# Turning y, k and q on VectorE instead of TensorE in the later units of an mLSTM cell with a feed-forward block

## Chip, cores and metric

The kernel runs on one core of a Trainium2 chip. The metric is the device time of one execution in microseconds (us), median of several runs. The profile is one further execution, taken by the hardware profiler; TensorE appears in it as PE (matmuls) and PEld (weight loads), VectorE as DVE, ScalarE as ACT, GpSimd as POOL, SyncE as SP. A q behind a name (SPq) is the sequencer of that engine, which issues DMAs.

## The reference, cut

```python
# q, k, v, o_gate: (4, 8, 768, 40); i_gate, f_gate: (4, 8, 768)
for t in range(S):
    m_new = np.maximum(f_gate[:, :, t] + m, i_gate[:, :, t])
    f_stab = np.exp(f_gate[:, :, t] + m - m_new); i_stab = np.exp(i_gate[:, :, t] - m_new); m = m_new
    C = f_stab * C + i_stab * outer(vt, kt)          # per batch and head, 40 x 40
    n = f_stab * n + i_stab * kt
    y[:, :, t] = sigmoid(o_gate[:, :, t]) * (C @ qt) / np.maximum(np.abs(n @ qt), 1.0)
x = y.transpose(0, 2, 1, 3).reshape(3072, 320)       # heads side by side
out = ((x @ w1) * (x @ w2) @ w3) @ w_out             # 320 -> 1024 -> 1024 -> 320
```

The activations are float32. The four weight matrices come as float64 and are turned into float32 on the core.

## The kernel before

**Units and steps.** The sequence of 768 is cut into 6 chunks of 128 rows; with 4 batches that gives 24 units (`NU`), unit n being chunk n // 4 of batch n % 4. In each unit the recurrence is done in matrix form for all 8 heads (two blocks of 64 rows, called halves in the code). The main loop runs over steps s = 0 to 29. Step s does the cell work of unit s, the outputs y of unit s - 1 and the feed-forward work of earlier units.

**Turning.** Rows of q, k and v lie with time on the partitions. The scores need k and q with the head dimension on the partitions: `turn(n)` (line 267) turns both on TensorE, four 128x128 transposes each into PSUM (tile `pt`), and ScalarE copies the result into `kT` and `qT`. One turned slab holds two heads, each padded from 40 to 64 rows; the padding columns of `qbuf` and `kbuf` are zero. The feed-forward block needs y turned in the same way: `x_trans(n)` (line 367) does three transposes on TensorE (tile `px`), and ScalarE copies them into `xT`, which holds a group of four units. Since 320 is 128 + 128 + 64, the last 64 columns are first doubled by GpSimd (`twice`, line 364) so that the 64-row remainder stands in both halves of the partitions.

**Cell.** `quarter_work(s)` (line 286) runs the cell matmuls of a step into one PSUM tile, `cell`, which has one buffer of four banks: the outputs of unit s - 1 from the weighted scores and v (`ph`) and from the old state and q (`pi`), then the state update of unit s (`pc`, from k and v) and its scores (`ss`, from kT and qT). The matmuls of 64 rows by 64 columns use the four quarters of the array (`quarters`). VectorE multiplies the scores by the weights (line 324, `first_read`), updates the states and calls `outputs(s - 1)` (line 341), which ends with y (line 361).

**Feed-forward.** `up` and `up_rest` (lines 493 and 506) form x @ w1 and x @ w2 for some of the eight blocks of 128 hidden columns (PSUM tiles `pa`, `pb`), ScalarE copies pa into `a_sb` (line 513), VectorE multiplies (line 514, tile `ab`). `ffn_out` (line 516) multiplies by w3 @ w_out, which has been formed once in `w3o` (`w3_mm`, tile `wp`); the result `po` is copied by ScalarE into `o_sb` (line 521) and stored by SP's queue (line 523). `n_up` and `n_down` say how many of each a step does: one `up` in steps 3 to 6, two in steps 7 to 28; two `ffn_out` in steps 17 to 26, four in step 29. Group gr, which is units 4 gr to 4 gr + 3, begins its ups at step 9 for gr = 1 and four steps later for each next one, and uses its last two units two steps after that.

**Weights.** `fetch` (line 185) loads a piece of raw words through SP's queue into one of four `raw` buffers (a piece of w3 takes four DMAs), ScalarE scales one half of the words (line 159), and `convert` (line 212) makes float32 of them in five VectorE operations (lines 170 to 174); pieces of w3 are also turned in 32x32 blocks by VectorE (line 223). `n_cvt` says how many conversions a step does, two in steps 9 to 15, the last. `fetched < converted + 3` keeps the fetches three pieces ahead.

**Order.** TensorE runs its instructions in the order in which the program names them (`in_order`). The other engines' and queues' order is set by the scheduler of the tile framework, within the dependencies. A tile with n buffers is reused after n allocations: `pt`, `px`, `wp`, `pa`, `pb` and `po` share the four buffers of the pool `ps_m`; after step 24 the space of `cell` is given back and becomes a second pool of four, and the two pools then take turns (`mps`, line 75). SP's queue carries, in each step, the broadcast weights `pw` of unit s + 3 (line 129), k, q and v of unit s + 2 (line 119), its output gate (line 123), the fetches and, from step 17 on, the output rows. A DMA that must wait for a buffer or for data holds up what is queued behind it.

Of the kernel before, what the change touches and what calls it, by code (L numbers as in the profile page):

```python
# [1 line left out]

# [6 lines left out]
FP = mybir.dt.float32  # L9
# [7 lines left out]
def kernel(  # L17
# [71 lines left out]
    def mm(out, lhsT, rhs, start=True, stop=True):  # L89
        in_order(nc.tensor.matmul(out, lhsT=lhsT, rhs=rhs, start=start, stop=stop))  # L90
# [2 lines left out]
        in_order(nc.tensor.transpose(out, in_, ident[0:n, 0:n]))  # L93

    halves = [slice(0, L), slice(L, P)]
    quarters = ((0, 0), (1, 1), (0, 1), (1, 0))


    NB, NBQ = 4, 3
    qbuf = [const.tile([P, H, DP], FP, name=f"qbuf{i}") for i in range(NBQ)]  # L100
    kbuf = [const.tile([P, H, DP], FP, name=f"kbuf{i}") for i in range(NB)]
    vbuf = [const.tile([P, H, D1], FP, name=f"vbuf{i}") for i in range(NB)]
# [4 lines left out]
    wT = const.tile([P, NT2, BH], FP, name="wT")  # L107
    decay = const.tile([P, B * NP, NT], FP, name="decay")
    U_d = dram.tile([NT, BH, L], FP, name="U_d")

    o_t, u_t = {}, {}

    def rows(src, n):
        c, b = divmod(n, B)
        return src[b, :, c * P:(c + 1) * P, :].rearrange("h p d -> p h d")

    def load(n):
        for dst, src in ((kbuf[n % NB][:, :, 0:D], k), (qbuf[n % NBQ][:, :, 0:D], q), (vbuf[n % NB][:, :, 0:D], v)):
            nc.sync.dma_start(out=dst, in_=rows(src, n))

    def load_o(n):
        o_t[n] = io.tile([P, H, D], FP, name="o_in", tag="o_in", bufs=4)
# [119 lines left out]
    qT_t, kT_t, vw_t, before_t, y_t, x_t = {}, {}, {}, {}, {}, {}  # L242
# [22 lines left out]
                                    pattern=[[0, H], [1, L]], channel_multiplier=-1)  # L265

    def turn(n):
        for src, dst, name in ((kbuf[n % NB], kT_t, "kT"), (qbuf[n % NBQ], qT_t, "qT")):
            pt = mps([128, NP, P], "pt")
            for p in range(NP):  # L270
                transpose(pt[:, p, :], src[:, 2 * p:2 * p + 2, :].rearrange("p a b -> p (a b)"))
            dst[n] = sb.tile([128, NP, P], FP, name=name, tag=name)
            nc.scalar.copy(out=dst[n], in_=pt)
# [12 lines left out]
    def quarter_work(s, rest):  # L286


        rest()
        t = ps_c.tile([P, 4, 512], FP, name="cell", tag="cell")  # L290

        def part(j, c0, n):
            return t[:, j:j + 2, c0:c0 + NP * n].rearrange("p x (n d) -> p x n d", d=n)

        ss, pc, pi = part(0, 0, L), part(0, NP * L, D1), part(2, 0, D1)
        ph = [t[halves[x], 2 + x, NP * D1:(NP + H) * D1].rearrange("p (h d) -> p h d", d=D1) for x in range(2)]
        n = s - 1
        if 0 <= n < NU:
            pw, vt, qT = u_t.pop(n), vbuf[n % NB], qT_t.pop(n)
            before = before_t.pop(n)  # L300
            for hd in range(H):
                for x, r in enumerate(halves):
                    mm(ph[x][:, hd, :], pw[r, hd, :], vt[r, hd, :])
            for p in range(NP):
                for hip, x in quarters:
                    mm(pi[halves[x], hip, p, :], qT[halves[hip], p, halves[x]], before[x][halves[hip], p, :])
        n, first_read = s, None
        if n < NU:
            c, b = divmod(n, B)
            kt, vw = kbuf[n % NB], vw_t.pop(n)  # L310
            ends = range(2 if c < NT2 - 1 else 1)
            first, second, after = state[b]
            before_t[n] = first, second
            state[b] = after, second, first
            for p in range(NP):
                for x, e in quarters:
                    if x in ends:
                        mm(pc[halves[e], x, p, :], kt[halves[x], 2 * p + e, :], vw[halves[x], 2 * p + e, :])
            kT, qT, pw = kT_t.pop(n), qT_t[n], u_t[n]
            for p in range(NP):  # L320
                for hip, x in quarters:
                    mm(ss[halves[x], hip, p, :], kT[halves[hip], p, halves[x]], qT[halves[hip], p, halves[x]])
            pv = pw.rearrange("p (n two) t -> p two n t", two=2)
            first_read = nc.vector.tensor_tensor(out=pv, in0=ss, in1=pv, op=OP.mult)  # L324
            with tc.issue_after(first_read.ins):

                if c:
                    nc.vector.tensor_tensor(out=second, in0=pc[:, 0], in1=second, op=OP.add)
                else:
                    nc.vector.tensor_copy(out=second, in_=pc[:, 0])  # L330
                if len(ends) > 1:
                    decayed(after, second, n, 1)
                    nc.vector.tensor_tensor(out=after, in0=pc[:, 1], in1=after, op=OP.add)
        if 0 <= s - 1 < NU:
            if first_read is None:
                outputs(s - 1, pi, ph)
            else:
                with tc.issue_after(first_read.ins):
                    outputs(s - 1, pi, ph)

    def outputs(n, pi, ph):
        c, b = divmod(n, B)
        hs = slice(b * H, (b + 1) * H)
        h = sb.tile([P, H, D1], FP, name="h", tag="h")
        nc.vector.tensor_tensor(out=h.rearrange("p (n two) d -> p two n d", two=2), in0=pi,  # L345
                                in1=gT[:, c, hs].rearrange("p (n two) -> p two n", two=2).unsqueeze(3)
                                .to_broadcast([P, 2, NP, D1]), op=OP.mult)
        for x, r in enumerate(halves):
            nc.vector.tensor_tensor(out=h[r], in0=ph[x], in1=h[r], op=OP.add)  # L349
# [11 lines left out]
        nc.vector.tensor_tensor(out=y_t[n][:, 0:DM].rearrange("p (h d) -> p h d", d=D), in0=h[:, :, 0:D], in1=e,  # L361
                                op=OP.mult)

    def twice(n):
        nc.gpsimd.tensor_copy(out=y_t[n][:, DM:DM + REM], in_=y_t[n][:, KF * P:DM])  # L365
# [12 lines left out]
    GR, GC = 3, NT // 3  # L378
    TC = GC * L
    RG = GR * BH  # L380
    f_sb, a, F, U, on = (const.tile([RG, TC], FP, name=n) for n in ("f_sb", "a", "F", "U", "on"))
    w, g = f_sb, on
    M = const.tile([RG, GC + 1], FP, name="M")
    dec = const.tile([RG, GC], FP, name="dec")
# [29 lines left out]
        nc.gpsimd.memset(vbuf[i][:, :, D:D1], 1.0)  # L414
    for t in state:
        nc.gpsimd.memset(t[0], 0.0)
    nc.gpsimd.memset(pick, 0.0)

    nc.vector.tensor_reduce(out=pair, in_=ident[0:RG, 0:RG].rearrange("k (g j x) -> k j g x", g=GR, x=2), op=OP.add,
# [96 lines left out]
    def ffn_out(gr, j):  # L516
        po = mps([P, DM], "po")
        for f in range(FO):
            mm(po, ab_t[gr][j // 2][:, f, j % 2 * P:(j % 2 + 1) * P], w3o[:, f, :], start=(f == 0), stop=(f == FO - 1))
        o_sb = ffn.tile([P, DM], FP, name="o_sb", tag="o_sb", bufs=3)  # L520
        nc.scalar.copy(out=o_sb, in_=po)  # L521
        t0 = j * S + gr * P
        nc.sync.dma_start(out=out[t0:t0 + P, :], in_=o_sb)


    ups = [(0, list(range(f, f + 4)), slice(j * P, (j + 1) * P)) for f in (0, 4) for j in range(GT)]
# [12 lines left out]
    for s in range(len(n_up)):  # L539
# [8 lines left out]
        if s < NU:  # L548
            weighted(s)
            if s >= B:  # L550
                decayed(state[s % B][1], state[s % B][0], s, 0)
            if s:
                turn(s)
        if 0 <= s - 2 < NU:
            twice(s - 2)
        while turned < min(s - 2, NU):
            x_trans(turned)
            turned += 1
        fold()
# [1 line left out]
            ffn_out(*downs.pop(0))  # L561
        now = [ups.pop(0) for _ in range(n_up[s])]
        open_ups = [up(*x) for x in now]
        if len(now) < 2 and turned == s - 2 < NU:
            x_trans(turned)
            turned += 1

        def rest():
            for x in open_ups:
                up_rest(*x)  # L570

        if s <= NU:
            quarter_work(s, rest)
# [53 lines left out]
```

## Time and profile before

| | us |
|---|---|
| median of 3 runs | 494.35 (494.25 to 498.0) |
| profiled execution | 495.68 |
| its span | 494.0 |
| around the span | 1.68 |

| group in the profile | count | busy us | mean ns |
|---|---|---|---|
| PE pt, from k and from q | 192 | 33.2 | 306 and 292 |
| PE px | 72 | 13.1 | 286 |
| ACT copies kT, qT, xT | 72 | 40.1 | 588, 595, 490 |
| POOL y (the doubling) | 24 | 7.3 | 306 |
| DVE block transpose of w3, 128x512 | 16 | 11.3 | 709 |
| PE cell, all forms | 3008 | 86.0 | 235 to 238 |

| DMA, all on SP's queue | count | KB each | median us to landing |
|---|---|---|---|
| k, q, v rows | 72 | 160 | 4.6, 4.9, 4.9 |
| output gate rows | 24 | 160 | 4.1 |
| raw words of w3 | 64 | 128 | 3.5 |
| output rows | 24 | 160 | 1.8 |

Busy time of a group adds up the durations of its instructions, also where several run at once; idle time is counted on the engine just before an instruction, with what ended it in brackets. The granted clock of TensorE is 1.00 at full speed. In a stretch of the span, the busy table gives how long each engine worked; an engine that is busy for the whole stretch sets its length.

### The profile page before, as it was taken

The page shows a single profiled execution, that of the slowest core. Times are in us where ns is not written, and L with a number is a line of the kernel's source. Part 1 is how long each engine was busy: PE and PEld are TensorE (multiplying, and loading weights), DVE is VectorE, ACT ScalarE, POOL GpSimd, SP SyncE. Part 2 cuts the span into 40 slices and gives each one's busy share as a digit, 9 for nine tenths or more (in the row PEclk, how much of TensorE's full clock was granted, in tenths as well). Part 3 has the DMA queues.
Part 4 walks back from the last instruction along what each step waited for, and adds up shares of the span by engine and source line. Part 5 has one row for each costly group of instructions (what it writes and reads, how often), then busy time and mean ns, then how long its engine had stood idle before and what let it go on. Part 6 is the DMA issues. An engine that isn't in the chain of part 4 may idle for free.

```text
span 494.0 us, 13423 instructions
## 1 busy us (share of the span) xinstructions
PE 462.7 (94%) x5714; PEld 380.6 (77%) x5714; DVE 247.5 (50%) x512; ACT 153.5 (31%) x413; POOL 88.6 (18%) x163
## 2 busy tenths in 40 slices
PE   3869797899899999999999999999999998999997
PEld 2759796898677888788878787777878777777864
DVE  7787688999877978977431331403214042111110
ACT  3743454533431543354331322412112011011011
POOL 5431223621311322212410211201000000000000
PEclk9989998989999999999999999999999999999999
DMA  9999936799877737543340422311000000000001
GB/s 186 169 196 197 155 91 130 124 184 180 156 147 136 156 113 152 103 74 56 53 88 15 102 50 56 65 40 41 15 28 1 27 16 15 27 15 13 1 15 40
DMA packets 115404, 42.33 MB, mean 86 GB/s; under 512 B 103120, under 2 KB 106384, under 8 KB 115344
## 3 DMA queue, kind: packets, MB, share of 16 engines
q1 hardware_dynamic: 115200, 41.37, 41.9%
q8 instruction: 45, 0.74, 0.7%
q14 instruction: 15, 0.12, 0.1%
q10 hardware_dynamic: 144, 0.10, 0.1%
HBM read 37.42 MB, written 4.03 MB: 84 GB/s over the span
## 4 chain that ended last, share of the span: by engine, by line
PE 75%; DVE 9%; issue 7%; DMA 3%; SPq 2%; POOL 2%; ACT 1%; DVEq 0%; POOLq 0%; ACTq 0%
PE po L90 21%; PE pa L90 20%; PE pb L90 14%; PE cell L90 7%; PE wp L90 7%; PE pt L93 3%; SPq L154 2%; DVE h L349 1%; DMA raw<-in_moe_w_dram 1%; DMA pw<-U_d 1%; PE px L93 1%; DMA kbuf<-in_k_dram 1%; PE ub L90 1%; DVE h L345 1%; DVE ma L173 1%
## 5 line engine op out<-in xcount | busy, mean ns | idle before, releaser
L514 DVE TENSOR_TENSOR ab<-pb,a_sb 128x512 f32<-128x512 f32 x48 | 33.0, 690 | 182.0 <-ACT a_sb L513 181.9
L90 PE MATMUL po<-w3o,ab 128*128 128x320 f32 x384 | 105.4, 433 | 1.3 <-DVE h L349 1.3
L90 PEld LDWEIGHTS po<-w3o,ab 128*128 128x128 f32 x384 | 72.2, 190 | 30.7 <-issue 1.5
L90 PE MATMUL pa<-xT,w 128*128 128x256 f32 (+1 forms) x448 | 93.0, 355 | 0.0
L90 PE MATMUL pb<-xT,w 128*128 128x256 f32 (+1 forms) x448 | 91.9, 351 | 0.4 <-issue 0.4
L90 PEld LDWEIGHTS pa<-xT,w 128*128 128x128 f32 x448 | 77.1, 195 | 10.7 <-ACT a_sb L513 0.8
L90 PEld LDWEIGHTS pb<-xT,w 128*128 128x128 f32 x448 | 76.3, 192 | 9.0 <-issue 0.6
L513 ACT ACTIVATE a_sb<-pa 128x512 f32<-128x512 f32 x48 | 28.6, 596 | 146.6 <-PE pb L90 146.6
L90 PE MATMUL pb<-xT,wr 64*64 64x256 f32 (+1 forms) x448 | 47.4, 351 | 0.0
L90 PE MATMUL pa<-xT,wr 64*64 64x256 f32 (+1 forms) x448 | 47.4, 351 | 0.0
L283 POOL TENSOR_TENSOR state<-state,decay 128x164 f32<-128x164 f32 x40 | 19.6, 493 | 154.2 <-PE cell L90 99.1
L264 POOL TENSOR_SCALAR_AFFINE_SELECT pw<-pw 64x512 f32<-64x512 f32 x48 | 36.9, 769 | 47.1 <-ACT pw L262 44.6
L262 ACT ACTIVATE pw<-pw,aT 128x64 f32<-128x64 f32 x160 | 40.6, 339 | 5.3 <-DMA pw<-U_d 5.3
L90 PEld LDWEIGHTS pa<-xT,wr 64*64 64x64 f32 x448 | 28.5, 133 | 14.9 <-issue 6.6
L90 PE MATMUL wp<-wo,w3T 128*128 128x320 f32 x128 | 35.9, 433 | 2.0 <-DVE w3T L223 2.0
L521 ACT COPY o_sb<-po 128x320 f32<-128x320 f32 x24 | 10.2, 426 | 74.8 <-PE po L90 74.7
L90 PEld LDWEIGHTS wp<-wo,w3T 128*128 128x128 f32 x128 | 23.7, 190 | 11.1 <-issue 2.2
L90 PEld LDWEIGHTS cell<-vbuf,pw 64*64 64x64 f32 x768 | 28.2, 145 | 2.8 <-issue 0.3
L90 PEld LDWEIGHTS pb<-xT,wr 64*64 64x64 f32 x448 | 28.5, 133 | 0.0
L90 PE MATMUL cell<-vbuf,pw 64*64 64x41 f32 x768 | 28.4, 235 | 0.0
L365 POOL COPY y<-y 128x64 f32<-128x64 f32 x24 | 7.3, 306 | 110.0 <-DVE y L361 109.8
L324 DVE TENSOR_TENSOR pw<-cell,pw 128x512 f32<-128x512 f32 x24 | 16.4, 685 | 19.0 <-PE cell L90 15.4
(89 smaller groups left out, 524.4 us busy)
## 6 DMA issues: line engine op xcount, KB each, us to landing
raw<-in_moe_w_dram SPq DMA_DIRECT2D x64, 128.0 KB, 3.5
pw<-U_d SPq DMA_DIRECT2D x40, 128.0 KB, 3.7
kbuf<-in_k_dram SPq DMA_DIRECT2D x24, 160.0 KB, 4.6
qbuf<-in_q_dram SPq DMA_DIRECT2D x24, 160.0 KB, 4.9
vbuf<-in_v_dram SPq DMA_DIRECT2D x24, 160.0 KB, 4.9
o_in<-in_o_gate_dram SPq DMA_DIRECT2D x24, 160.0 KB, 4.1
out_dram<-o_sb SPq DMA_DIRECT2D x24, 160.0 KB, 1.8
raw<-in_moe_w_dram SPq DMA_DIRECT2D x7, 512.0 KB, 5.8
```

What stands on the lines that cost most here:

```text
L90: in_order(nc.tensor.matmul(out, lhsT=lhsT, rhs=rhs, start=start, stop=stop))
L93: in_order(nc.tensor.transpose(out, in_, ident[0:n, 0:n]))
L154: nc.sync.dma_start(out=dst, in_=src)
L173: V.scalar_tensor_tensor(out=r.bitcast(FP), in0=lo, scalar=2.0 ** -52, in1=r.bitcast(FP), op0=OP.mult, op1=OP.mult)
L262: nc.scalar.activation(out=pw[:, h, :], in_=src[:, h, :], func=AF.Exp, bias=aT[:, c, b * H + h:b * H + h + 1])
L264: nc.gpsimd.affine_select(out=pw[r], in_=pw[r], compare_op=OP.is_ge, fill=0.0, base=0, pattern=[[0, H], [1, L]], channel_multiplier=-1)
L283: nc.gpsimd.tensor_tensor(out=new, in0=old, op=OP.mult, in1=decay[:, b * NP:(b + 1) * NP, 2 * c + x:2 * c + x + 1] .to_broadcast([P, NP, D1]))
L324: first_read = nc.vector.tensor_tensor(out=pv, in0=ss, in1=pv, op=OP.mult)
L365: nc.gpsimd.tensor_copy(out=y_t[n][:, DM:DM + REM], in_=y_t[n][:, KF * P:DM])
L513: nc.scalar.mul(out=a_sb, in_=pa, mul=UP ** -2)
L514: nc.vector.tensor_tensor(out=ab_t[gr][j][:, fs[0]:fs[-1] + 1, t0:t0 + a_sb.shape[-1]], in0=pb, in1=a_sb, op=OP.mult)
L521: nc.scalar.copy(out=o_sb, in_=po)
```

## The change

- From unit 8 on (`NY`), y is not turned by TensorE. `send(n)` stores y to DRAM in pieces of 32 floats (four DMAs), `get_back(n)` loads it again with the 32-column blocks spread over the partitions (four DMAs, tile `yb`), and `x_turn(n)` turns it in 32x32 blocks on VectorE straight into `xT`. The remainder is stored twice, which takes the place of `twice`.
- From unit 17 on (`N_DVE`), k and q are not turned by TensorE. `load_turned(n)` loads both once more, each partition holding four time rows of 160 bytes behind one another for each pair of heads, and each of the four quarters of the partitions holding all 32 such groups of one head of the pair, shifted by 32 columns in every second quarter (eight DMAs), and `turn(n)` is two block transposes on VectorE, made a step ahead, behind the outputs. q's ordinary load is left out for these units; k's stays, for the state update.
- The matmuls from kT, qT and the state use 40 rows of each half (`heads`) and not 64, in all units.
- The tiles of the gate computation become slices of one tile, `gates`, which later holds the raw k and q; GpSimd fills two parts of it with zeros.
- Output rows are stored through ScalarE's queue; `o_sb` has two buffers and not three.
- Fetches stay two pieces ahead from step 9 on, and three before.
- The turn of y of unit 0 moves from step 2 to step 3 (`len(now) == 1` in place of `len(now) < 2`).

```diff
+    heads = [slice(0, D), slice(DP, DP + D)]
+    N_DVE = 17
+    NY = 8
+    KC = KF + 1
+    y_d = [dram.tile([P, 4, KC, 32], FP, name=f"y_d{n}") if n >= NY else None for n in range(NU)]
...
+            if src is not q or n < N_DVE:
+                nc.sync.dma_start(out=dst, in_=rows(src, n))
+    def load_turned(n):
+        c, b = divmod(n, B)
+        for dst, src in zip(turned_in, (k, q)):
+            for hip in range(2):
+                of = src[b].rearrange("(p two) s d -> two p s d", two=2)[hip, :, c * P:(c + 1) * P, :]
+                for j in range(2):
+                    p0, c0 = hip * DP + j * 32, (1 - j) * 32
+                    nc.sync.dma_start(out=dst[p0:p0 + 32, c0:c0 + NP * RAW].rearrange("r (p e) -> r p e", p=NP),
+                                      in_=of.rearrange("p (r f) d -> p r (f d)", f=4))
...
     def turn(n):
+        if n >= N_DVE:
+            for src, dst, name in zip(turned_in, (kT_t, qT_t), ("kT", "qT")):
+                dst[n] = sb.tile([128, NP, P], FP, name=name, tag=name)
+                nc.vector.transpose(out=dst[n].rearrange("i p (r f) -> i p f r", f=4),
+                                    in_=src[:, 32:TB].rearrange("i (p f d) -> i p f d", p=NP, f=4)[:, :, :, 0:32])
+            return
...
-                    mm(pi[halves[x], hip, p, :], qT[halves[hip], p, halves[x]], before[x][halves[hip], p, :])
+                    mm(pi[halves[x], hip, p, :], qT[heads[hip], p, halves[x]], before[x][heads[hip], p, :])
...
-                    mm(ss[halves[x], hip, p, :], kT[halves[hip], p, halves[x]], qT[halves[hip], p, halves[x]])
+                    mm(ss[halves[x], hip, p, :], kT[heads[hip], p, halves[x]], qT[heads[hip], p, halves[x]])
...
+    def send(n):
+        y = y_t.pop(n)
+        for cc in range(KF):
+            nc.sync.dma_start(out=y_d[n][:, :, cc, :], in_=y[:, cc * P:(cc + 1) * P].rearrange("t (i c) -> t i c", c=32))
+        for i in range(0, 4, 2):
+            nc.sync.dma_start(out=y_d[n][:, i:i + 2, KF, :], in_=y[:, KF * P:DM].rearrange("t (i c) -> t i c", c=32))
+    def get_back(n):
+        back_t[n] = sb.tile([P, 4, KC, 32], FP, name="yb", tag="yb", bufs=1)
+        for i in range(4):
+            nc.sync.dma_start(out=back_t[n][32 * i:32 * (i + 1)].rearrange("r m k c -> r m (k c)"),
+                              in_=y_d[n][:, i].rearrange("(m r) k c -> r m (k c)", r=32))
+    def x_turn(n):
+        gr, j = divmod(n, GT)
+        if j == 0:
+            x_t[gr] = ffn.tile([128, KC, TG], FP, name="xT", tag="xT")
+        nc.vector.transpose(out=x_t[gr][:, :, j * P:(j + 1) * P].rearrange("c k (m r) -> c k m r", r=32),
+                            in_=back_t.pop(n).rearrange("r m k c -> r k m c"))
...
-    f_sb, a, F, U, on = (const.tile([RG, TC], FP, name=n) for n in ("f_sb", "a", "F", "U", "on"))
+    gates = const.tile([P, 2 * TB], FP, name="gates")
+    f_sb, a, F, U, on = (gates[0:RG, i * TC:(i + 1) * TC] for i in range(5))
+    turned_in = [gates[:, i * TB:(i + 1) * TB] for i in range(2)]
...
-        o_sb = ffn.tile([P, DM], FP, name="o_sb", tag="o_sb", bufs=3)
+        o_sb = ffn.tile([P, DM], FP, name="o_sb", tag="o_sb", bufs=2)
-        nc.sync.dma_start(out=out[t0:t0 + P, :], in_=o_sb)
+        nc.scalar.dma_start(out=out[t0:t0 + P, :], in_=o_sb)
...
-            if s:
+            if 0 < s < N_DVE:
                 turn(s)
-        if 0 <= s - 2 < NU:
+        if NY <= s - 2 < NU:
+            send(s - 2)
+        elif 0 <= s - 2 < NY:
             twice(s - 2)
-        while turned < min(s - 2, NU):
+        if N_DVE <= s + 1 < NU:
+            load_turned(s + 1)
+        if NY <= s - 2 < NU:
+            get_back(s - 2)
+        while turned < min(s - 2, NY):
             x_trans(turned)
...
-        if len(now) < 2 and turned == s - 2 < NU:
+        if len(now) == 1 and turned == s - 2 < NY:
...
+        with tc.issue_after(gated.ins) if gated else nullcontext():
+            if NY <= s - 2 < NU:
+                x_turn(s - 2)
+            if N_DVE <= s + 1 < NU:
+                turn(s + 1)
...
-        while todo and fetched < converted + (2 if s < 2 else 3):
+        while todo and fetched < converted + (3 if 2 <= s < 9 else 2):
```

`gated` is the last instruction of the outputs (y), which `quarter_work` now returns.

More of the change, by code (lines that the diff above doesn't have):

```diff
@@ L1 @@
-from contextlib import ExitStack
+from contextlib import ExitStack, nullcontext
 import concourse.bass as bass
@@ L118, in load @@
         for dst, src in ((kbuf[n % NB][:, :, 0:D], k), (qbuf[n % NBQ][:, :, 0:D], q), (vbuf[n % NB][:, :, 0:D], v)):
-            nc.sync.dma_start(out=dst, in_=rows(src, n))
+            if src is not q or n < N_DVE:
[8 more added lines that the diff above has]
+                    nc.sync.dma_start(out=dst[p0:p0 + 32, c0:c0 + NP * RAW].rearrange("r (p e) -> r p e", p=NP),
+                                      in_=of.rearrange("p (r f) d -> r p (f d)", f=4))
     def load_o(n):
@@ L335, in quarter_work @@
             if first_read is None:
[L336 to L339, printed above, removed]
+                return outputs(s - 1, pi, ph)
+            with tc.issue_after(first_read.ins):
+                return outputs(s - 1, pi, ph)
     def outputs(n, pi, ph):
@@ L360, in outputs @@
         y_t[n] = sb.tile([P, DM + REM], FP, name="y", tag="y")
-        nc.vector.tensor_tensor(out=y_t[n][:, 0:DM].rearrange("p (h d) -> p h d", d=D), in0=h[:, :, 0:D], in1=e,
+        return nc.vector.tensor_tensor(out=y_t[n][:, 0:DM].rearrange("p (h d) -> p h d", d=D), in0=h[:, :, 0:D], in1=e,
                                 op=OP.mult)
+    def send(n):
[4 more added lines that the diff above has]
+            nc.sync.dma_start(out=y_d[n][:, i:i + 2, KF, :], in_=y[:, KF * P:DM].rearrange("t (i c) -> t i c", c=32))
+    back_t = {}
+    def get_back(n):
[9 more added lines that the diff above has]
+                            in_=back_t.pop(n).rearrange("r m k c -> r k m c"))
     def twice(n):
@@ L380 @@
     RG = GR * BH
-    f_sb, a, F, U, on = (const.tile([RG, TC], FP, name=n) for n in ("f_sb", "a", "F", "U", "on"))
+    RAW = 4 * D
+    TB = 32 + NP * RAW
+    gates = const.tile([P, 2 * TB], FP, name="gates")
+    f_sb, a, F, U, on = (gates[0:RG, i * TC:(i + 1) * TC] for i in range(5))
+    turned_in = [gates[:, i * TB:(i + 1) * TB] for i in range(2)]
     w, g = f_sb, on
@@ L416 @@
         nc.gpsimd.memset(t[0], 0.0)
+    nc.gpsimd.memset(gates[:, 5 * TC:2 * TB], 0.0)
+    nc.gpsimd.memset(gates[RG:P, NP * RAW:TB], 0.0)
     nc.gpsimd.memset(pick, 0.0)
@@ L570, in rest @@
                 up_rest(*x)
+        gated = None
         if s <= NU:
-            quarter_work(s, rest)
+            gated = quarter_work(s, rest)
         else:
             rest()
+        with tc.issue_after(gated.ins) if gated else nullcontext():
[3 more added lines that the diff above has]
+                turn(s + 1)
         if s == 0:
```

## Prediction

> **What bounds the kernel now.** I read the busy line first.
>
> ```profile
> PE 462.7 (94%) x5714; PEld 380.6 (77%) x5714; DVE 247.5 (50%) x512; ACT 153.5 (31%) x413; POOL 88.6 (18%) x163
> ```
>
> An average over the span hides the stages, so next the busy table by stretch (busy us of PE, PEld, DVE, ACT, POOL, then the granted clock, the DMA share and GB/s).
>
> ```profile
> 33.80:61.00 27.20, 23.81 (x538) 21.94 (x539) 18.54 (x40) 11.41 (x31) 5.06 (x10) 0.88 0.99 180
> 61.00:129.20 68.20, 60.64 (x1152) 57.03 (x1151) 62.39 (x132) 31.86 (x90) 23.10 (x38) 0.93 0.74 146
> 129.20:252.30 123.10, 121.95 (x1549) 99.79 (x1550) 91.99 (x185) 48.85 (x135) 29.41 (x46) 1.00 0.57 113
> 252.30:418.00 165.70, 165.70 (x1735) 131.90 (x1734) 39.49 (x89) 34.86 (x84) 14.25 (x28) 1.00 0.16 37
> ```
>
> Up to 129 us no engine is full: DMA is saturated until 61, then VectorE is (62.4 of 68.2). From 129 us on TensorE is never idle for more than 1.2 us until 418; that is steps 10 to 24. There every matmul that goes away shortens the span, if nothing new makes TensorE wait. The chain of waits over one step shows what each item weighs on that path (start, us, what).
>
> ```profile
> 244.53 2.32 PE cell L90 x123
> 246.84 1.02 PE pt L93 x8
> 247.87 0.33 PE px L93 x3
> 248.19 4.31 PE wp L90 x16
> 252.50 8.61 PE po L90 x32
> ...
> 269.91 2.32 PE cell L90 x123
> 272.23 1.02 PE pt L93 x8
> 273.25 0.33 PE px L93 x3
> ```
>
> A step costs 16.77 us up to step 16 and 21.08 from step 17 on (273.58 - 252.50), all of it TensorE; pt (k and q turned) is 1.02 of it and px (y turned) 0.33. The busy sums (306 ns a transpose) would overstate both, since transposes overlap; the chain's share is what leaves.
>
> **What is removed.** pt leaves for units 17 to 23. Their turns are the first work of steps 17 to 23 and start at 246.84, 272.23 and so on to 377.60, all inside the full stretch: 7 x 1.02 = 7.1 us. px leaves for units 8 to 23, at steps 11 to 26, all after 147 us. Fifteen of them are worth 0.33: 5.0 us. Unit 22's stands where TensorE does wait (timeline, with the idle time before a row in brackets):
>
> ```profile
> 417.85 0.55 PE L93 MATMUL px<-ident,y 128*128 128x128 f32 x3
> 418.53 1.01 DVE L349 TENSOR_TENSOR h<-cell,h 64x328 f32<-64x328 f32 x2
> 419.69 2.66 PE L90 MATMUL po<-w3o,ab 128*128 128x320 f32 x9 [1.29 <-DVE h L349]
> ```
>
> At step 25 the two PSUM pools alternate, the old one first. px takes the old pool, so the first po gets the space of `cell`, and waits until VectorE has read it. Without px the first po takes the old pool and starts at once; the second, 4.3 us later, finds `cell` read. Bounds: 0.3 (the wait merely moves) to 1.8 (419.69 - 417.85); I take 1.7, since the order of pools is fixed in the code. Removed in all: 7.1 + 5.0 + 1.7 = 13.8 us. ScalarE's copies (595, 588, 490 ns) and GpSimd's (306 ns) leave too, off the path.
>
> **What is moved at the front.** Unit 0's px goes from step 2 to step 3. In step 2 TensorE idled 4.06 us before it, for y of unit 0, with the cell work of unit 2 behind it. VectorE's reads of the previous cell end at 31.1, so that work could start there, not at 34.6; but VectorE is converting until 36.6 and takes the result then, not at 39.2. Bounds: 0 (DMA share 0.99 in this stretch holds the later loads where they are) to -2.6. I take -1.0, nearer to the saturated row.
>
> **What is added.** VectorE: one block transpose of 128x384 per unit from 8 on, two of 128x512 from 17 on. The row for that operation:
>
> ```profile
> L223 DVE STREAM_TRANSPOSE w3T<-w 128x512 f32<-128x512 f32 x16 | 11.3, 709 | 0.5
> ```
>
> So 0.53 us (709 x 384/512) to 0.71 a step, then 1.42 more; with strides no row shows, at most I double it. In steps 10 to 15 VectorE is busy 12.6 to 13.7 us of 16.8, so 14.4 of 16.4 after: hidden, if its inputs are there. From step 17 on it is busy under 6 of 21. The turns stand behind y of the unit before, and the next who waits for VectorE is ab, whose rows were preceded by 1.6 to 3.0 us of idle time in those steps; kT and qT are needed a step later, xT one or more.
>
> SP's queue: per unit from 8 on, four stores of y, a wait until they have landed, four loads; behind that wait stand the fetches of weight words and the next step's loads. The queue now, in one step:
>
> ```profile
> 153.60 1.09 SPq L129 DMA_DIRECT2D pw<-U_d  x2
> 154.74 0.59 SPq L119 DMA_DIRECT2D kbuf<-in_k_dram  x1
> 155.37 0.58 SPq L119 DMA_DIRECT2D qbuf<-in_q_dram  x1
> 156.05 1.05 SPq L119 DMA_DIRECT2D vbuf<-in_v_dram  x1
> 157.20 0.83 SPq L123 DMA_DIRECT2D o_in<-in_o_gate_dram  x1
> 158.13 7.55 SPq L154 DMA_DIRECT2D raw<-in_moe_w_dram  x8
> ```
>
> The loads take 4.4 us; eight fetches take 3.5 when not blocked (four took 1.74 at 203.66), the rest of the 7.55 is a wait for buffers that the shorter look-ahead removes. Stores and loads of y: 4 x 0.43 each, 1.7 + 1.7. The landing: 1.8 as for the output rows, or, behind four loads still moving, 4.9 as for v plus 2.8 for its own packets (512 + 512 + 256 + 256 = 1,536; queue 1 spent 41.9% of 16 x 494 us on 115,200, 28.7 ns each, over 16 engines); 4.5 is between, near to the loads' rows of 4.1 to 4.9, the same mix. Sum: 4.4 + 1.7 + 4.5 + 1.7 + 3.5 = 15.8 of a 16.44 us step; ends 13.1 and 19.0. At the upper end the queue falls behind by 2.6 us in each of steps 10 to 14, 13 us, of which VectorE's idle time and the queue's lead of some 2 us at the turns take half. Cost on the path: 0 to 6, taken 1.0. From step 16 on there are no fetches but eight raw loads of k and q (8 x 0.43 = 3.4, less 0.6 for q): 15.1 of 19.7, hidden.
>
> The Trainium skill ("DMA: Bandwidth & Descriptors", Specifications) speaks against this route: below 512 bytes a transfer makes the DMA read, modify and write. The y stores are of 128 bytes. If that doubled a packet's time, their own 2.8 us would be 5.5, an estimate from that page, the queue 18.5 a step and my sum some 4 us higher; no row of this trace writes pieces of 128 bytes.
>
> TensorE once stood 1.15 us at 145.2 for nothing the profile names, with the DMA share near 1; more traffic may bring another such: 0 to 2, taken 0.3. Output rows by ScalarE: 24 issues of 0.37 to 0.5 us behind their own copies, with ScalarE busy 6 of 21 us a step; 0. Two o_sb buffers: a copy follows the one two before by 8.6 us, a row lands in 1.8; 0. Two fills on GpSimd, which waits 2.72 us there: 0. Without that cover, 0.3.
>
> **Sum.** -13.8 - 1.0 + 1.0 + 0.3 = -13.5. The profiled execution took 495.68 (span 494.0 and 1.68 around it), 1.3 above the median; the difference is applied to the median: 494.35 - 13.5 = 480.9, say 481.
>
> **Rivals.** (a) SP's queue sets the step in steps 10 to 14, by the upper end above: half and more of the gain stays, 481 + 6 = 487. For it: DMA share 0.53 to 0.73 there already, one queue. Against: its lead, and VectorE's idle time.
>
> (b) Slower: the score and state matmuls now contract 40 rows for 64, in all units. Today four quarters run at once: 32 such matmuls take 0.47 us, 15 ns each. The one form that is not 64 or 128 rows, the 96-row ub, took 1.10 us for 32, 34 ns each. If 40-row tiles cease to share the array, 64 matmuls x 19 ns = 1.2 us a unit, 18 over the 15 units in the full stretch and 29 over all: 481 + 18 to 481 + 29, 499 to 510. It decides from 0.9 us a unit on over 15 units (13.5 / 15). Against: start partitions stay 0 and 64, and 96 rows cannot fit a half.
>
> (c) VectorE, in order, stands at the turns in every step from 10 to 25 because data lands late (the single buffer of raw k and q is refilled only after the last turn). Loop: 3.4 of issue + 4.9 to land + 1.4 of turning = 9.7 against 19.7, so it should not; if the landing took three times as long, TensorE would lose about 1 us a step, 16 us: 497.
>
> **Chances.** Forecast 0.74 (478 to 484), (a) 0.13 (484 to 490), (b) 0.06, (c) 0.07. The range 478 to 489 takes in the front's -2.6 and nearly all of (a), and leaves out (b) and (c). One per cent is 4.9 us, about what a measurement of this kernel can tell. Faster by more (under 489.4): 0.74 and 0.11 of (a), 0.85; within it: 0.02 of (a) and 0.05 of (c), 0.07; slower: (b) and 0.02 of (c), 0.08.
>
> **What would show it.** Right: steps 17 to 23 of 19.7 us with cell followed by po at once; steps 11 to 16 of 16.4; no idle time at step 25. Wrong: idle rows of TensorE or ab on y, yb, kT or xT; SP's fetches landing after VectorE wants them; cell longer than 2.32 us a step.

## The result and the profile after

| | before | after |
|---|---|---|
| median of 4 runs, us | 494.76 (494.25 to 498.0) | 508.77 (506.1 to 510.37) |
| ratio | 1 | 1.0264 [1.0209, 1.0319] |
| profiled execution, and its span, us | 495.68, 494.0 | 510.37, 508.6 |
| first wp (step 10), first po (step 17), end of last po, us | 129.2, 252.3, 490.6 | 130.1, 275.8, 505.4 |

The kernel became slower by 14.0 us where 13.5 us of gain were forecast. The busy line of the profile after:

```profile
PE 461.2 (91%) x5610; PEld 375.5 (74%) x5610; DVE 268.6 (53%) x542; ACT 139.2 (27%) x383; POOL 85.8 (17%) x149
```

TensorE has 104 matmuls fewer and only 1.5 us less busy time, and no engine became full: something makes TensorE wait, and run slower. Where, is told by the last row of the table above. The front lost 0.9 us, the steps from the first wp to the first po lost 22.6 (145.7 for 123.1), and the rest gained 8.7 (229.6 for 238.3). The busy table by stretch of the kernel after (columns as before) for the same first stretch as in the prediction, and then for its own stretch from first wp to first po:

```profile
129.20:252.30 123.10, 112.18 (x1325) 89.54 (x1326) 83.80 (x169) 37.10 (x98) 23.73 (x33) 0.94 0.63 116
...
130.10:275.80 145.70, 127.69 (x1520) 101.32 (x1521) 97.05 (x193) 43.04 (x118) 29.14 (x39) 0.92 0.58 108
```

TensorE, which was busy for 121.95 of 123.10 us before, now idles 18.0 of 145.7, and its granted clock fell from 1.00 to 0.92: it was busy for 5.7 us more, though seven px (of units 8 to 14, 7 x 0.33) and the pt of unit 17 (1.02) had left, 3.3 us by the prediction's prices. So of the 25.9 us that go missing there against a stretch shortened by those 3.3, some 17 are idle time and some 9 slower matmuls.

The late steps are another matter. The chain of waits over one of them (start, us, what):

```profile
296.29 8.81 PE po L90 x32
...
313.89 2.32 PE cell L90 x123
316.21 3.97 PE po L90 x14
```

po follows the cell at once, nothing stands between them, and a step takes 19.92 us (316.21 - 296.29) for 21.08. At step 25 the row of po in the timeline has no wait in front of it:

```profile
434.10 0.67 PE L90 MATMUL cell<-state,qT 40*64 40x41 f32 x30
434.69 2.69 PE L90 MATMUL po<-w3o,ab 128*128 128x320 f32 x9
```

So the loss lies in steps 10 to 17. The table of waits of the kernel after for that stretch (who waited for whom: us in total, times, longest):

```profile
PE wp L90 <- DVE den L377: 14.9, 2, 8.0
DVE ex L186 <- ACT raw L175: 11.4, 4, 5.3
PE wp L90 <- DVE w3T L239: 4.5, 3, 2.0
```

The two rows of that kind in the kernel before:

```profile
PE wp L90 <- DVE w3T L223: 2.0, 1, 2.0
...
DVE ex L170 <- ACT raw L159: 1.5, 1, 1.5
```

In both kernels one wait of 1.98 us in wp's rows ends at the first wp, and so lies just ahead of the stretch. wp is the product that forms a slice of w3o; it reads w3T, the result of a weight conversion. `den` has nothing to do with it: it ends next to the transposition of w3T (below, 225.68 + 0.71 = 226.39, wp at 226.53), and the wait is put down to what ended last. The timeline around the longest waits:

```profile
216.07 0.69 DVE L568 TENSOR_TENSOR ab<-pb,a_sb 128x512 f32<-128x512 f32 x1 [6.38 <-ACT a_sb L567]
216.68 0.42 DVE L188 TENSOR_SCALAR ma<-ex 128x512 uint32<-128x512 uint32 x1
...
225.68 0.71 DVE L239 STREAM_TRANSPOSE w3T<-w 128x512 f32<-128x512 f32 x1
226.53 6.12 PE L90 MATMUL wp<-wo,w3T 128*128 128x320 f32 x16 [6.94 <-DVE den L377]
232.68 0.44 ACT L255 ACTIVATE w3o<-wp 128x320 f32<-128x320 f32 x1 [11.81 <-PE wp L90]
233.02 1.23 ACT L175 ACTIVATE raw<-raw 128x512 f32<-128x512 f32 x2
233.71 0.43 DVE L186 TENSOR_SCALAR ex<-raw 128x512 uint32<-128x512 uint32 x1 [5.29 <-ACT raw L175]
```

It reads as a ring. wp waits for VectorE's conversion; ScalarE's copy of w3o waits 11.81 us for wp; the scales of the next raw words stand behind that copy in ScalarE's order; VectorE waits 5.29 us for them to begin the conversion that the next wp needs. And VectorE stood idle for 6.38 us in the middle of a conversion, because ab, which waits for TensorE, stands in its order ahead of the conversion's third operation. Each link is an engine that takes its instructions in a fixed order. The words themselves had been there: of the eight DMAs of those two pieces the last seven were issued from 210.31 to 213.6, and they take 3.2 us to land (median), so by 217 us; ScalarE scaled them at 233.02.

The lead that was lost can be counted in the two traces. From the end of the second half of w3T to the start of its wp it was, in steps 12 to 17, 6.7 to 10.5 us before (236.77 + 0.71 to 248.03, for one); after, 4.3 us in step 12 and 0.1 in each step from 13 on: every wp starts the moment its conversion is done. The rows of the kernel before for that one:

```profile
236.77 0.71 DVE L223 STREAM_TRANSPOSE w3T<-w 128x512 f32<-128x512 f32 x1
...
248.03 4.20 PE L90 MATMUL wp<-wo,w3T 128*128 128x320 f32 x15
```

SP's queue, whose fullness the prediction had feared, in one of these steps (start, us of issue):

```profile
178.29 1.85 SPq L392 DMA_DIRECT2D y_d<-y  x2
180.19 1.15 SPq L394 DMA_DIRECT2D y_d<-y  x2
181.44 1.36 SPq L170 DMA_DIRECT2D raw<-in_moe_w_dram  x1
189.29 1.74 SPq L401 DMA_DIRECT2D yb<-y_d  x4
191.07 3.26 SPq L170 DMA_DIRECT2D raw<-in_moe_w_dram  x7
```

From 182.8 to 189.29 it issues nothing: the loads of yb wait until VectorE has turned the unit before (xT at 188.70, yb has one buffer), and the fetches stand behind them.

### The profile page after: what moved, and what is told of

It reads as the page before. It is cut to its first block, busy times and chain, and to the rows that moved or that the text cites. A ratio compares the mean times of both kernels' runs of the same rounds, so it can differ in the third digit from the quotient of the medians.

```text
span 508.6 us, 13461 instructions
## 1 busy us (share of the span) xinstructions
PE 461.2 (91%) x5610; PEld 375.5 (74%) x5610; DVE 268.6 (53%) x542; ACT 139.2 (27%) x383; POOL 85.8 (17%) x149
## 3 DMA queue, kind: packets, MB, share of 16 engines
q1 hardware_dynamic: 147344, 47.18, 48.7%
q10 hardware_dynamic: 3600, 4.03, 2.3%
HBM read 44.01 MB, written 7.18 MB: 101 GB/s over the span
## 4 chain that ended last, share of the span: by engine, by line
PE 73%; DVE 11%; issue 9%; POOL 2%; DMA 2%; SPq 1%; ACT 1%; DVEq 0%; POOLq 0%
PE po L90 21%; PE pa L90 20%; PE pb L90 14%; PE wp L90 9%; PE cell L90 6%; DVE h L372 2%; DVE ma L189 1%; PE pt L93 1%; POOL state L307 1%; DMA kbuf<-in_k_dram 1%; PE ub L90 1%; SPq L170 1%; DVE w L190 1%; DVE ab L568 1%; DVE h L368 1%
## 5 line engine op out<-in xcount | busy, mean ns | idle before, releaser
L90 PE MATMUL pa<-xT,w 128*128 128x256 f32 (+1 forms) x448 | 95.3, 362 | 0.6 <-ACT xT L422 0.6
L90 PEld LDWEIGHTS pa<-xT,w 128*128 128x128 f32 x448 | 79.4, 202 | 11.7 <-ACT xT L422 1.0
L90 PE MATMUL wp<-wo,w3T 128*128 128x320 f32 x128 | 43.8, 504 | 19.9 <-DVE den L377 14.9
L307 POOL TENSOR_TENSOR state<-state,decay 128x164 f32<-128x164 f32 x40 | 21.0, 526 | 200.6 <-PE cell L90 71.1
L90 PEld LDWEIGHTS wp<-wo,w3T 128*128 128x128 f32 x128 | 28.0, 224 | 33.4 <-issue 25.3
L90 PEld LDWEIGHTS cell<-vbuf,pw 64*64 64x64 f32 x768 | 27.1, 140 | 4.2 <-issue 2.0
L90 PE MATMUL cell<-vbuf,pw 64*64 64x41 f32 x768 | 27.0, 229 | 1.4 <-issue 1.4
L372 DVE TENSOR_TENSOR h<-cell,h 64x328 f32<-64x328 f32 x48 | 23.8, 496 | 1.0
```

The source lines that it names most:

```text
L307: nc.gpsimd.tensor_tensor(out=new, in0=old, op=OP.mult, in1=decay[:, b * NP:(b + 1) * NP, 2 * c + x:2 * c + x + 1] .to_broadcast([P, NP, D1]))
```

## The experiments

Three theories were stated at first: (1) the single buffer of yb holds the fetches up; (2) the shorter look-ahead leaves VectorE without words; (3) the y route itself costs, by its traffic of many small pieces. A time below that is not called a median is that of one execution; six executions of one kernel lay between 484.2 and 489.0 us, so differences of 2 or 3 us between single times say little. The stretches come from the traces.

**More buffers for yb.** Only the place of the tile is changed; the traces show the same order of work on VectorE and ScalarE in steps 10 to 17.

```diff
-        back_t[n] = sb.tile([P, 4, KC, 32], FP, name="yb", tag="yb", bufs=1)
+        if n < NY + 6:
+            c0 = n % 3 * DP * 6
+            back_t[n] = gates[:, c0:c0 + 4 * KC * 32].rearrange("p (m k c) -> p m k c", m=4, k=KC)
+        else:
+            back_t[n] = sb.tile([P, 4, KC, 32], FP, name="yb", tag="yb", bufs=1)
```

> Units 8 to 13 get their turned-back y (yb) in three places of the tile `gates`, which is unused between the gate computation and step 16, instead of the one yb buffer; nothing else changes, and the order on every engine stays. Theory 1 (the load of y back waits for the one yb buffer, that is for the turn of the unit before on VectorE, and holds up the fetches of weight words behind it on SP's queue): the fetches are issued right after the stores have landed, TensorE no longer waits before wp, the first po starts at about 252 us and not 276, and the time is 485 us (483 to 489): 494.8 less 8.7 measured from step 17 on and 2.0 for six px, plus 0.9 lost at the front. Rival 2 (the shorter look-ahead of the fetches starves VectorE): no change, 503 to 510. Rival 3 (the DMA traffic of y, many small pieces, makes everything land late): no change or a few us, 500 to 510.

It took 512.06 us. The loads of yb for units 9 to 11 started 7 to 14 us sooner (161.13, 176.18 and 194.61 for 168.56, 189.29 and 208.53), the fetches behind them as well, and nothing came of it: wp waited 14.9 us in two places and 6.6 in four more, ex 10.4 for raw. The buffer and the landing of the words alone are not the cause; with the same order on the engines the loss stayed. Theory 1 had expected 483 to 489.

**The old look-ahead.**

```diff
-        while todo and fetched < converted + (3 if 2 <= s < 9 else 2):
+        while todo and fetched < converted + (2 if s < 2 else 3):
```

> The changed kernel with the old look-ahead, three pieces from step 2 on. Theory 1: the fetches still stand behind the load of y, but one piece (half a step's need) is fetched earlier, so a part comes back: 495 to 505. Rival 2 (look-ahead): nearly all comes back, 484 to 489. Rival 3 (traffic): no change, 505 to 510.

501.47 us: half of the loss. wp's waits shrank to 5.0 in three, none above 2.0, and a new one appeared. The timeline of this kernel in step 13:

```profile
189.49 0.70 DVE L239 STREAM_TRANSPOSE w3T<-w 128x512 f32<-128x512 f32 x1
190.12 0.45 DVE L384 TENSOR_TENSOR y<-h,o_in 128x320 f32<-128x320 f32 x1
190.49 0.56 DVE L408 STREAM_TRANSPOSE xT<-yb 128x384 f32<-128x384 f32 x1
191.20 3.54 PE L90 MATMUL pa<-xT,w 128*128 128x256 f32 x8 [3.59 <-DVE xT L408]
```

pa now waits for the turn of y. VectorE's fixed order shows why: the turn of unit 9 stands behind y of unit 11, which stands behind a conversion. The program writes the turn of unit n behind y of unit n + 1; the scheduler put it one step later. The first matmuls of the cell of step 12 start at 177.84, the turn follows 12.7 us later, but TensorE has only pt and wp to do before it wants it. In the kernel after, this lateness is hidden by the longer wait of wp ahead of pa.

**The fetches ahead of the stores of y.** The fetches of a step are issued before `send` from step 10 on, with the new look-ahead.

```diff
+        if s >= 10:
+            while todo and fetched < converted + (n_cvt[s] if s < len(n_cvt) else 0) + 2:
+                fetch(*todo.pop(0))
+                fetched += 1
         if NY <= s - 2 < NU:
             send(s - 2)
```

> The changed kernel with the fetches of a step placed ahead of the stores of y on SP's queue from step 10 on; one yb buffer, look-ahead of two after the step as in the changed kernel. Theory 1: the wait for yb now holds up only the next loads of k, q and v, which have more than a step of slack: 485 to 490. Rival 2: no change, 503 to 510, since no piece more is in flight at a step's end. Rival 3: 500 to 510.

507.41 us. wp waited 2.0 us in all; pa waited 16.6 for xT, 10.3 of it at once: in VectorE's order the turn had moved behind one conversion more. One wait was exchanged for the other.

**y on TensorE, all else of the change.**

```diff
-    NY = 8
+    NY = NU
```

> The changed kernel with y turned on TensorE in all units as before (no y through DRAM); k and q turned on VectorE from the 18th unit on, 40-row matmuls, ScalarE's queue for the output rows, look-ahead of two. Theory 1: no wait for yb; the seven pt leave, 7 x 1.0, plus 0.9 at the front: 488.5 (487 to 491). Rival 2 (look-ahead): still slow, 500 to 505. Rival 3: 488.5 too, since the traffic of y is gone.

491.39 us, 3.4 under the kernel before, with first wp to first po in 123.0 us and steps of 20.20 from step 18 on; theories 1 and 3 had expected 488.5, theory 2 at least 500. Without the y route the new look-ahead, the 40-row matmuls and the output rows cost nothing that shows: the cell takes 2.32 us as before, and the one wait of wp is again the 1.98 us that ends at the first wp.

None of the three theories had held alone: theory 1 fails on the first and third run, theory 2 on the second and fourth, theory 3 on the second. What was left: two waits that hide each other, both from the fixed orders. (A) the turn of y stands a step late on VectorE; (B) with fetches both called late and held up by y's transfers, the scales and conversions stand where they need TensorE's next result. Three runs were made to tell this apart.

**y on VectorE only after the conversions.**

```diff
-    NY = 8
+    NY = 16
```

> The changed kernel with VectorE turning y from the 17th unit on (NY = 16) instead of the 9th; units 8 to 15 go back to TensorE and ScalarE. No y goes through DRAM while w3's words are still converted (steps 10 to 15). Theory (the loss needs the y route and the conversions in the same steps, because VectorE takes both in one order): the loss is gone. Against 491.4 with y wholly on TensorE, the units 16 to 22 lose their px, 7 x 0.33 = 2.3 us, and step 25 its wait of 1.7: 486 to 489 us, w3o's products at 4.3 to 4.5 us without a wait. Rival (the y route costs TensorE something wherever it runs, by its 128-byte stores and loads): at least 491.4, and steps of over 20.2 us from step 18 on.

485.32 us. The row of the busy table from its first wp to its first po, and the only wait of wp, which ends at the first wp and so stands just ahead of that row:

```profile
129.70:251.00 121.30, 121.17 (x1542) 99.00 (x1543) 90.69 (x185) 47.33 (x129) 30.09 (x46) 1.00 0.58 114
```

```profile
PE wp L90 <- DVE w3T L239: 3.6, 1, 3.6
```

TensorE is busy for all of it at full clock. The loss needs the y route and the conversions in the same steps.

**The turn of y where the program writes it.** One order is added on VectorE, all else as in the change.

```diff
+            with tc.issue_after(last_turn[-1].ins) if last_turn else nullcontext():
-            first_read = nc.vector.tensor_tensor(out=pv, in0=ss, in1=pv, op=OP.mult)
+                first_read = nc.vector.tensor_tensor(out=pv, in0=ss, in1=pv, op=OP.mult)
```

Here `last_turn` holds the latest turn of y; the lines that set it are left out.

> The changed kernel with one order added on VectorE: the cell's first product of step s+1 stands behind the turn of unit s-2, so that the turn of unit n comes at the end of step n+2, where the program writes it, and not behind the conversions and y of step n+3. Look-ahead, fetches and stores as in the change. Theory A (the turn's place in VectorE's order is the loss: TensorE's pa wants xT 6 us after the cell, VectorE turns it 12 us after): no pa waits for xT, yb's loads and the fetches behind them come a step sooner, 484 to 491 us. Theory B (the fetches called two pieces ahead come late, so ScalarE's scales stand behind the copy of w3o, and VectorE's conversions behind ab): wp still waits 2 to 8 us for w3T and the time stays at 500 or above.

504.09 us; the ring is still there, in the timeline:

```profile
222.75 0.54 DVE L410 STREAM_TRANSPOSE xT<-yb 128x384 f32<-128x384 f32 x1
222.97 6.34 PE L90 MATMUL wp<-wo,w3T 128*128 128x320 f32 x16 [5.28 <-DVE w3T L239]
229.35 0.44 ACT L255 ACTIVATE w3o<-wp 128x320 f32<-128x320 f32 x1 [10.39 <-PE wp L90]
229.69 1.23 ACT L175 ACTIVATE raw<-raw 128x512 f32<-128x512 f32 x2
```

The turn now stands ahead of wp, and pa waits for xT nowhere; wp waits 16.6 us in six places for w3T (1.98 of it ahead of the first wp). Theory A alone falls.

**Both: that order and the old look-ahead.** The two edits are those shown above.

> As the run with the added order, and in addition the look-ahead of before (3 pieces from step 2 on). That look-ahead without the order took 501.5 us, with two waits of 3.5 us of pa for xT. Theory A alone: like the run with the order alone, within 2 us. A and B together (each of the two must be put right): 484 to 488 us here, and 4 us or more above this in the run with the order alone. If VectorE's time as such is the limit in steps 10 to 15 (two conversions of 7 us in all, the turn and the rest in a step of 16.4 us), it stays above 495 in both.

489.39 us, 14.7 under the run with the order alone and 12.1 under the one with the look-ahead alone. Its waits and its busy row from first wp to first po:

```profile
PE wp L90 <- DVE w3T L239: 6.5, 3, 3.6
...
PE pa L90 <- DVE xT L410: 1.2, 2, 0.7
```

```profile
129.50:255.40 125.90, 120.20 (x1521) 96.88 (x1522) 93.31 (x186) 42.92 (x118) 27.12 (x39) 1.00 0.67 124
```

The first of the three waits, of 3.62 us, again ends at the first wp. The traces show what the look-ahead does to the order: with the old one VectorE's order has three conversions, and not two, between its first reads of the cell in steps 10 and 11 (`first_read`), and from then on it stays one conversion further ahead. So the y route fits beside the conversions if both orders are put right, with VectorE busy for 93.3 of 125.9 us; but only just, for in steps 13, 15 and 17 wp still starts some 0.15 us after its w3T. It was 1.4 us above the range that A and B together gave, and it gains nothing against leaving y on TensorE there: 125.9 us for 123.0. The stretch from first wp to first po in all of them (the times of the first two are medians):

| kernel | A put right | B put right | stretch, us | time, us |
|---|---|---|---|---|
| before (no y route) | | | 123.1 | 494.76 |
| after | no | no | 145.7 | 508.77 |
| turn where written | yes | no | 140.2 | 504.09 |
| old look-ahead | no | yes | 135.9 | 501.47 |
| both | yes | yes | 125.9 | 489.39 |
| y route after the conversions | not needed | not needed | 121.3 | 485.32 |

The two do not add: 5.5 and 9.8 us alone, 19.8 together, as waits do that hide each other.

**The front's line alone**, beside y on TensorE.

```diff
-        if len(now) == 1 and turned == s - 2 < NY:
+        if len(now) < 2 and turned == s - 2 < NY:
```

> As the run in which TensorE turns all of y (491.4 us), with the one line of the front put back (x_trans of the step's unit also where a step has no up products, so that unit 0 is turned in step 2). It measures that edit by itself. The prediction had the changed line at a gain of 1.0 us; if so this run takes 492.4. If the changed line costs what the changed kernel shows (first wp 0.9 us late where 1.0 early was expected), this run takes 489.5 to 490.5, with the first wp before 129.5 us.

491.02 us for 491.39, first wp at 129.9: neither expectation, and inconclusive. In these runs the first wp lay anywhere between 127.8 and 131.2 us in kernels with the changed line and between 129.2 and 132.1 in kernels with the old one, so an edit of 1 us there can't be read from one profile.

**Candidates, timed.** First y from the 17th unit on with the old line of the front, then that with the old look-ahead too, then y from the 17th unit on by itself.

> The run with y on VectorE from the 17th unit on (485.3 us), with the old line of the front put back, which by itself took 0.4 us off the kernel with all of y on TensorE. Expected 484.5 to 485.5 us if the two add; ratio to before 0.978 to 0.982. If VectorE's late turns of y are only free by chance of one profile, the runs of this kernel spread and the median goes above 488.

> As the run above, and the look-ahead of before (3 pieces). With y on VectorE only after the conversions, the look-ahead should matter little: theory B says that fetches called late hurt only where y's loads and turns stand in their way. In the run without the old look-ahead one wait of 3.6 us of w3o's products for w3T is left (2.0 in before), so at most 3.6 us can come of it: 481 to 485 us. If it is slower than the run above by over 1 us, the shorter look-ahead has a use of its own.

> The kernel with y on VectorE from the 17th unit on, once more, now timed in rounds. One look gave 485.3 us, the same with the old line of the front 486.9 to 489.9 in four. If the line of the front matters, this lies at 485 to 486.5; if the 2.4 us between the two are the spread of runs, its median lies at 486 to 488. In both cases a ratio to before of 0.978 to 0.985.

Medians 487.76 (486.9 to 489.86), 488.23 (486.83 to 489.32) and 487.08 (484.23 to 489.0); ratios to before 0.9831 [0.9769, 0.9893], 0.9829 [0.9757, 0.9901] and 0.9807 [0.9768, 0.9847]. They can't be told apart: once the y route starts after the conversions, no effect of the front's line or of the look-ahead stands out of the spread, and the single 485.32 lies low in it. The first two are slower than expected. All three medians and their intervals lie below the kernel before, and so below the one after; whether the gain reaches 2% is open for each. The third is the change with a single number altered.

**k and q on TensorE beside the late y route.**

```diff
-    N_DVE = 17
+    N_DVE = NU
```

> The run with y on VectorE from the 17th unit on (485.3 us), with k and q turned by TensorE in every unit (N_DVE = 24). It measures the turning of k and q beside the late y route. The prediction had it at 7 x 1.02 = 7.1 us: then 492.4 here. The steps of the traces say 0.88 for each (21.08 to 20.20): then 491.5. If VectorE has no room for k, q and y together in the late steps, the run is under 490.

491.06 us: turning k and q on VectorE is worth 4.0 us against the median of 487.08 (5.7 against the single run), below the forecast of 7.1; the steps give 7 x 0.88 = 6.2 (20.20 us for 21.08), and the rest is within the spread of single runs. y from the 17th unit on is worth 491.39 - 487.08 = 4.3 us; the expectation was 4.0.

Not tried: y on VectorE from the 9th unit on with k and q on TensorE; the turn put where the program writes it together with the fetches ahead of the stores; the scales forced ahead of the copy of w3o with the new look-ahead, which would test the one link of ring B by itself.

## Why the prediction was wrong

- **The step that failed** is the costing of the added y turns in steps 10 to 15: "14.4 of 16.4 after: hidden, if its inputs are there", with "kT and qT are needed a step later, xT one or more": the turns were put at nothing, and all that the y route might cost was booked on SP's queue, "Cost on the path: 0 to 6, taken 1.0". It compared busy time with the length of a step, and asked of the queue only whether it is full. Measured were 25.9 us. VectorE's busy time fits (93.3 of 125.9 us with both orders right); what did not fit is the place in the order. The margin of "one step or more" was used up by the scheduler's putting the turn a step later, behind two conversions. The idle time ahead of ab, which it read as 1.6 to 3.0 us, is 0.72 and 0.89 in the rows of steps 13 and 14. And it never set down how early w3T came to wp: 6.7 to 10.5 us in the kernel before, which had to cover all that the change puts ahead of it, and did not.
- **The look-ahead was booked as a relief**: "the rest of the 7.55 is a wait for buffers that the shorter look-ahead removes", which freed 4 us of the queue. It had no price of its own. It was harmless by itself (491.39 us with y on TensorE), but together with the y route it is one of the two halves of the loss.
- **SP's queue** was sized nearly right and was not the bound. Measured: loads 4.3 for 4.4, stores of y 3.0 for 1.7, loads of yb 1.74 for 1.7, fetches 4.6 for 3.5, landing 1.9 to 2.6 for 4.5. It idled 6.5 us in the step shown. Rival (a) named the right place with the wrong mechanism, and its upper end was a quarter of the loss.
- **Rival (c)** was nearest in kind, VectorE held in order, but had it stand at the turns for data that land late. In this stretch VectorE waited for yb nowhere; TensorE waited for VectorE. Its price was 16 us over steps 10 to 25, which its own loop does not give (with the landing tripled 3.4 + 14.7 + 1.4 = 19.5 of 19.7); the loss was all in 10 to 17.
- **Rival (b)** did not come: the cell takes 2.32 us a step as before.
- **Late steps: mechanism right, sizes a little off.** Forecast were 19.73 us a step (21.08 less 1.35), measured 19.92. pt is worth 0.88 a step (21.08 to 20.20), not the 1.02 that the chain gave it; px 0.28 (20.20 to 19.92), not 0.33. What comes right behind the cell takes 0.15 to 0.20 us longer on the chain: px 0.48 for 0.33 where only pt is gone, po 8.81 for 8.61 where both are. That makes up the difference; its cause is open.
- **Step 25**: right, the wait of 1.29 us is gone.
- **The front** (-1.0 forecast): open, since its spread is larger.
- **The traffic** (+0.3 for unnamed stalls): the prediction's test case on 128-byte pieces, which the Trainium skill ("DMA: Bandwidth & Descriptors", Specifications) says are read, modified and written, shows no such cost here. The DMA rows of the kernel after (KB each, median us to landing):

```profile
yb<-y_d SPq DMA_DIRECT2D x64, 48.0 KB, 1.9
...
y_d<-y SPq DMA_DIRECT2D x32, 64.0 KB, 2.6
y_d<-y SPq DMA_DIRECT2D x32, 32.0 KB, 1.9
```

The trace has 24,576 packets of 128 bytes on that queue, the y stores alone, at 13.4 ns on average; its packets of 160 bytes took 19.5. The written bytes grew from 4.03 to 7.18 MB, which is y alone (16 x 128 x 384 x 4 bytes = 3.15 MB), and the mean packet of the main queue took 26.9 ns (48.7% of 16 x 508.6 us on 147,344) after 28.7 before.

## What to carry over

Before work is moved onto an engine with idle time, find in the trace who needs that engine's results and how early each of them comes now; that lead, not the idle time of the engine, is what the added work may use up. Where engines run in a fixed order, an added operation costs by where it stands and by what then stands behind it; look at that order, and expect that a shorter look-ahead that is free by itself may cost beside a longer route in the same queue. When a change loses, put one half right at a time and then both: two waits that hide each other make each repair look weak.

## What was not expected of the hardware

A wait of TensorE can cost more than its length. The busy table of the kernel after for the wp that followed the wait of 6.94 us (columns for PE alone: busy, granted clock, DMA share, GB/s):

```profile
226.40:232.50 6.10, 5.97 (x17) 0.73 0.19 44
```

The sixteen matmuls took 6.12 us instead of the 4.47 to 4.54 of undisturbed rows, at a granted clock of 0.73. The Trainium skill ("TensorE: Matmul & The Clock Gate", Why this matters for your kernels) asks for no idle gaps above some 3 us. In these runs the waits of 3.59, 5.28, 6.94 and 7.96 us were followed by slow matmuls, but two waits of about 2 us were too (1.98 and 2.03 in the kernel after, wp 6.24 each), while others of 1.98, 2.03 and even 3.62 us were not (wp 4.54). The same wait of 1.98 us ahead of the first wp, first in the kernel after, then in the one before:

```profile
130.00:136.30 6.30, 6.23 (x17) 0.73 0.85 179
...
129.10:133.60 4.50, 4.41 (x17) 1.00 0.82 176
```

The clock recorded in the traces shows what decides. It changes only at multiples of 3.41 us: in the kernel after it is 1.00 until 130.72, 0.50 until 134.14, and 1.00 again until 185.34, fifteen times 3.41 later. Counted over the 14 traces from 110 to 478 us, a period of 3.41 us at full clock in which TensorE neither multiplied nor loaded weights for 1.95 us or more was followed by one at 0.50 in 19 of 20 cases; where that time was 1.89 or less, in none. The wait of 1.98 us lay whole in one period in the kernel after (127.31 to 130.72) and was cut in two in the kernel before, 0.72 and 1.23 us. The price of one such period here is 6.24 - 4.54 = 1.70 us, half of 3.41.

The block transposes on VectorE differ in how they write (group rows: busy, mean ns):

```profile
L239 DVE STREAM_TRANSPOSE w3T<-w 128x512 f32<-128x512 f32 x16 | 11.3, 708 | 0.4
L408 DVE STREAM_TRANSPOSE xT<-yb 128x384 f32<-128x384 f32 x16 | 9.1, 568 | 18.8 <-DMA yb<-y_d 18.8
L289 DVE STREAM_TRANSPOSE kT<-gates 128x512 f32<-128x512 f32 x7 | 7.6, 1079 | 0.0
```

kT, whose output goes to every fourth element, took 1079 ns for the same 512 columns as w3T with 708; within the doubling that was allowed. It also reads blocks of 32 out of rows of 40, so that the write is the cause is not shown apart from the read.
